# Staging four pairs of attention heads in the room of a later weight matrix: the third and fourth pair brought forward in a fused attention and two-layer expert kernel

## The chip, the cores and the metric

The kernel runs on one core of one Trainium2 chip. The metric is the device time of one execution in microseconds (us), smaller being better; a comparison takes the median of several executions.

## The reference, cut to what matters

```python
def _attn_ref(q, k, v):                      # q, k, v: 4 x 8 x 576 x 64
    scores = scale * np.matmul(q, k.transpose(0, 1, 3, 2))
    kth = np.partition(scores, -top_k, axis=-1)[..., -top_k:-top_k + 1]   # top_k = 32
    scores = np.where(scores >= kth, scores, -1000000000.0)
    attn = softmax(scores)
    return np.matmul(attn, v)
def _moe_ref(x, w_in, w_out):                # x: 2304 x 512, w_in 512 x 2048
    return softplus(x @ w_in) @ w_out
def _moe2_ref(x, w_gate, w1, w2):            # 8 experts, the best one for each token
    return gate * (np.maximum(x @ w1[e], 0) @ w2[e])
```

## The kernel before

The program has three parts that follow and overlap one another: attention with the 32 largest scores of each row kept, a dense layer pair (softplus between the two products), and a layer pair per expert with the tokens sorted by their expert.

**Attention** works on pairs of heads. A pair's q, k and v (each 128 x 576 in float32, 288 KB) are loaded by `load`, called from `prep_load` (L328). `prep_split` (from L375) makes of each a half-precision value and its remainder: ScalarE copies (L386, L406), VectorE or GpSimd subtracts (L387, L407). k and q are then turned by DMA transposes (L389, L392), q is swapped into a second tile by two DMAs (L394, L395), and v is spread over its tile by six DMAs (L411 to L413, twice). ScalarE also sums the magnitudes of each (L343). Pairs 0 to 3 are the four pairs of the first batch and go through `prep_split`; later pairs go through `prep_step` (L440 to L457), a third of a pair at a time. "Pair 2" and "pair 3" below are the third and fourth.

The first four pairs need room that the kernel does not have for long. The weight matrix `w_out_s` (16 blocks of 512 columns in float32) is filled only later, so `load` puts the raw inputs of pair 1 from its block 12 and of pair 2 from its block 8 (`ROOM`), and `staging` puts the halves of pair 1 from its block 4 (`STROOM`). Pairs 0 and 3 use the raw tiles of the pool `raw` (one set, so pair 3's loads wait for pair 0's split, and pair 4's for pair 3's); pairs 0, 2 and 3 use the staging tiles of the pool `stg` (one set, so each waits for the transposes and copies of the one before).

A **group** is two tiles of 128 query rows. PE computes its scores in two pieces (L479, tiles sa and sb), ScalarE copies them out (L489, L525), VectorE folds them and finds the 32nd largest by rounds of MAX8 and MATCH_REPLACE8 (L519 to L545), ScalarE and GpSimd make the exponentials (L552 to L565: Relu with the threshold L553, subtraction L554, Exp L555, half-precision copy L563, remainders L564 and L565), a DMA transpose turns the result (L567, tile pT), and three groups later PE multiplies it with v (L582, L584) and VectorE divides (L606 to L609). There are 72 groups; groups 0 and 1 belong to pair 0, groups 2 and 3 to pair 1, groups 4 and 5 to pair 2, groups 6 and 7 to pair 3.

**The dense layers' weights** arrive as 64-bit numbers and are decoded in 32 blocks (`decode`): a load by SP (L234, two buffers), ScalarE L243 and L247, VectorE L245 and L248, GpSimd L249, and for w_in also L254 to L256. A list `dec_q` holds the blocks in order; `decode_some(n)` takes the next n at a chosen priority. The dense layers run in units of two tiles (L669 first product, L706 and L709 second); a unit starts when the rows of x it needs are done, turned by a DMA transpose (L631, tile xT).

**The order of the work** is not written out. The program text gives each piece a priority (`tc.high_priority(offset=...)`, and `tc.issue_after(x)` holds a piece back until x has been issued), and a scheduler with a timeline of its own lays out one fixed sequence for each engine and for the queue of SP, which issues nearly all DMAs. Each engine then runs its sequence strictly in that order, waiting at an instruction until what it needs is there.

The main loop takes i from -1. At i = -1 it loads pairs 0 and 1, splits those whose time has come, and decodes two blocks; at each later i it emits group i's selection and decodes four blocks (`DECR`). After pair 0's split the loads of pairs 2 and 3 are emitted behind pair 0's last q transpose; after pair 3's split those of pair 4.

Of the kernel before, what the change touches and what calls it, by code (L numbers as in the profile page):

```python
# [19 lines left out]
B, H, S, D = 4, 8, 576, 64  # L20
NT, DM, DFF = 2304, 512, 2048
E, F2 = 8, 1024
R = 9
# [25 lines left out]
SWEEPS = [((0, 1), (8, 2, 3))] * 3 + [((0, 1), (8, 2), (3,))]  # L49
UNITS = [[(b,2*i),(b,2*i+1)] for b in range(3) for i in range(2)]+[[(0,'tail0')],[(3,0),(3,1)],[(3,2),(1,'tail1')],[(3,3)]]  # L50
ROOM = {1: 12, 2: 8}
STROOM = 4
V_NOW = 1
XB = 1
FLB = 4
# [20 lines left out]
DECR = 4  # L76
# [9 lines left out]
A_PREP = 150  # L86
# [110 lines left out]
def part_one(tc, ctx, q, k, v, w_in, w_out, const, ident, before, ones, iota_e, reg_e, wg, ids,  # L197
# [80 lines left out]
    def clear_table():  # L278
        fill = w_out_s[:, KF - 1, DM - (E * NT + SLOT) // 128:].bitcast(I32)
        nc.gpsimd.iota(fill, pattern=[[0, (E * NT + SLOT) // 128]], base=TRASH, channel_multiplier=0)  # L280
        nc.sync.dma_start(table.rearrange("(p a) o -> p (a o)", p=128), fill)
# [28 lines left out]
    def decode_some(n):  # L310
        for _ in range(n):
            if dec_q:
                f, *a = dec_q.pop(0)
                f(*a)


    pair, raws, last_t, last_l = {}, {}, {}, [None]
# [3 lines left out]
    def load(m, i):  # L321
        b, hp = pairs[m]
        if flags is not None and m in ROOM:
            a = ROOM[m] * DM + i * R * D
            t = w_out_s.rearrange("p k c -> p (k c)")[:, a:a + R * D]
        else:
            t = raw.tile([128, R * D], F32, name="qkv"[i] + "n")
        last_l[0] = nc.sync.dma_start(t, (q, k, v)[i][b, 2 * hp:2 * hp + 2].rearrange("h (p r) d -> (h p) (r d)", r=R))  # L328
        pair[m][0][i] = t

    def prep_load(m):
        src = [None] * 3
        bd = sm.tile([128, 3], F32, name="bd") if flags is None else sums[:, m]
        pair[m] = raws[m] = (src, bd)
        for i in range(3):
            load(m, i)
        if flags is None:
            magnitudes(m, stg.tile([128, R * D], F16, name="st"))

    def magnitudes(m, junk):  # L340
        src, bd = raws[m]
        for i, t in enumerate(src):
            nc.scalar.activation(junk, t, AF.Abs, accum_out=bd[:, i:i + 1])  # L343

    def prep_scale(m):
        b = pairs[m][0]
        src, bd = pair[m]
        if flags is not None:
            return
        up, iv = pow2(all_sum(bd, ps_m, "m"), "m")  # L350
        sc = sm.tile([128, 8], F32, name="sc", bufs=KVB + 2)
        nc.vector.tensor_copy(sc[:, 0:3], up)
        nc.vector.tensor_tensor(out=v_up[:, b:b + 1], in0=v_up[:, b:b + 1], in1=up[:, 2:3], op=ALU.min)
        nc.vector.scalar_tensor_tensor(sc[:, 3:4], iv[:, 0:1], 1.0 / D ** 0.5, iv[:, 1:2],
                                       op0=ALU.mult, op1=ALU.mult)
        nc.vector.tensor_scalar(sc[:, 4:5], sc[:, 3:4], -1.0, None, op0=ALU.mult)
        for i in (1, 0, 2):
            nc.scalar.activation(src[i], src[i], AF.Copy, scale=sc[:, i:i + 1])
        pair[m] = (*src, sc)

    def staging(m, i):
        cols = 2 * D + 2 if i == 2 else 2 * D
        if flags is not None and m == 1:
            a = STROOM * DM * 2 + i * R * 2 * D
            st = w_out_s.rearrange("p k c -> p (k c)").bitcast(F16)[:, a:a + R * cols]
            st = st.rearrange("p (r c) -> p r c", c=cols)
        elif i == 2:
            st = stg.tile([128, R, cols], F16, name="vs")
        elif i and m < ST0:
            st = row.tile([128, R, 2, D], F16, name="p16", bufs=PB if flags is not None else 2)  # L370
        else:
            st = stg.tile([128, R, 2, D], F16, name="st")
        return st if i == 2 or len(st.shape) == 4 else st.rearrange("p r (s d) -> p r s d", d=D)

    def prep_split(m):  # L375
        qn, kn, vn, sc = pair[m] if flags is None else (*pair[m][0], None)
        sub = nc.vector if m < DVS else nc.gpsimd
        q1 = kv.tile([128, 2, R, D], F16, name="q1")
        q2 = kv.tile([128, 2, R, D], F16, name="q2")
        kt = kv.tile([128, R, 128], F16, name="kt")  # L380
        if flags is not None and m >= LATEJ:
            magnitudes(m, q2[:, 0].rearrange("p r d -> p (r d)"))
        for i, xs in enumerate((kn, qn)):
            xv = xs.rearrange("p (r d) -> p r d", d=D)
            st = staging(m, i)
            nc.scalar.activation(st[:, :, 0, :], xv, AF.Copy)  # L386
            sub.tensor_tensor(out=st[:, :, 1, :], in0=xv, in1=st[:, :, 0, :], op=ALU.subtract)  # L387
            if i == 0:
                nc.sync.dma_start_transpose(out=kt, in_=st.rearrange("p r s d -> p (r s d)"))  # L389
            else:  # L390
                for h in range(2):
                    last_t[m] = nc.sync.dma_start_transpose(  # L392
                        out=q1[:, h], in_=st[64 * h:64 * h + 64].rearrange("p r s d -> p (r s d)"))
        nc.sync.dma_start(q2[0:64], q1[64:128])  # L394
        nc.sync.dma_start(q2[64:128], q1[0:64])  # L395
        pair[m] = q1, q2, kt, vn, sc
        if V_NOW:
            prep_v(m)
# [321 lines left out]
    def some_work(k):  # L720
        for _ in range(k):
            moe_step()
            if side:
                next(side[0], None)
                if side[0].gi_frame is None:
                    side.pop(0)
# [115 lines left out]
    for b, hp, ts in visits:  # L842
# [3 lines left out]
        m = len(pairs) - 1 - pairs[::-1].index((b, hp))  # L846
# [22 lines left out]
    done_prep, to_scale = 0, []  # L869
    credit, started = 0, 0  # L870
    for i in range(-1, n + LAG):
        if i == -1:
            with tc.high_priority(offset=2 * A_PREP):
                for m in range(RB if flags is None else 2):
                    with ExitStack() as loads_in_order:
                        if m:
                            loads_in_order.enter_context(tc.issue_after(last_l[0].ins))
                        prep_load(m)
                prep_scale(0)
        for m, step in steps.get(i, []):  # L880
            with tc.high_priority(offset=A_PREP):
                prep_step(m, step)
        while done_prep < whole and when[done_prep] <= i:
            with tc.high_priority(offset=A_PREP):
                if to_scale:
                    prep_scale(to_scale.pop()[0])
                prep_split(done_prep)
                if flags is None:
                    if done_prep + RB < len(pairs):
                        prep_load(done_prep + RB)  # L890
                elif done_prep in (0, 3):
                    if done_prep:
                        prep_load(4)
                    else:
                        with tc.issue_after(last_t[0].ins):
                            prep_load(2)
                            prep_load(3)
                if done_prep + 1 < len(pairs):
                    to_scale.append((done_prep + 1, i + SCALE))
            done_prep += 1  # L900
        if to_scale and to_scale[0][1] <= i:
            with tc.high_priority(offset=AHEAD):
                prep_scale(to_scale.pop()[0])
        if i == -1:
            with tc.high_priority(offset=A_PREP), ExitStack() as behind_q:
                behind_q.enter_context(tc.issue_after(last_t[0].ins))
                decode_some(2)
            clear_table()
        if i + 1 < n:
            with tc.high_priority(offset=A_SC):  # L910
                emit_scores(i + 1)
        if 0 <= i < n:
            with tc.high_priority(offset=AHEAD):
                emit_softmax(i)
            with tc.high_priority(offset=0):
                decode_some(DECR)
        j = i - LAG
        if j >= 0:
            with tc.high_priority(offset=A_AV), ExitStack() as behind_scores:
                if i + 1 < n:  # L920

                    behind_scores.enter_context(tc.issue_after(last_qk[0].ins))
                for x in groups[j]:
                    emit_av(*x)
            for u in units.get(j, []):
                started += 1
                ready.append((u, started))
        if ready or cur or behind or side:
            credit += MOER
            some_work(int(credit))  # L930
            credit -= int(credit)
# [270 lines left out]
```

## Time and profile before

| | us |
|---|---|
| median of 3 runs | 1059.6 (1058.11 to 1059.95) |
| the profiled execution | 1056.08 |
| its span, first to last instruction | 1054.1 |
| PE busy in the span | 886.1 (84%) |
| VectorE (DVE) busy | 851.3 (81%) |
| ScalarE (ACT) busy | 802.2 (76%) |
| GpSimd (POOL) busy | 602.0 (57%) |
| first selection (L519) starts | 19.36 |
| a group's first MAX8 (L529) starts, first and last | 21.8 and 688.7 |
| dense layers' first product (L669) starts, first and last | 147.8 and 809.5 |

The shares are means over parts with different limits. In the first 250 us VectorE, ScalarE and GpSimd are nearly always busy and PE mostly waits; from 300 us PE is busy nine tenths of the time and more, to the end. The profiled execution was 3.5 us under the median; the parts of a sum are taken from it and compared with its own time.

### The profile page before, as it was taken

What the parts mean: (1) busy time and instruction counts of PE and PEld (TensorE: products, weight loads), DVE (VectorE), ACT (ScalarE), POOL (GpSimd) and SP (SyncE); (2) the same over time, 40 slices, a digit from 0 to 9 for tenths busy, and PEclk for the clock granted to TensorE, in tenths of its full rate; (3) what the DMA queues carried; (4) which work ended last, traced back from release to release, by engine and by line L of the source; (5) the groups of instructions that cost most, each with busy time, mean ns of one, the idle gap of its engine ahead of it and who ended that gap; (6) DMA issues with size and microseconds to landing.
All of it is one profiled execution on the core that took longest, in us unless ns stands there. A gap on an engine that the chain in (4) does not pass through costs nothing.

```text
span 1054.1 us, 22206 instructions
## 1 busy us (share of the span) xinstructions
PE 886.1 (84%) x7146; PEld 657.8 (62%) x7146; DVE 851.3 (81%) x3021; ACT 802.2 (76%) x1866; POOL 602.0 (57%) x631
## 2 busy tenths in 40 slices
PE   2124359775999998998999899999999999999995
PEld 1013246444766666665667566676787899999993
DVE  4879999898989798996998999955457887777774
ACT  5879889989879898997997898863678455555553
POOL 3789989898768787876787677661001022111111
PEclk9965569886999998998999999999999999999998
DMA  8897889977698996769879456465101667766760
GB/s 198 204 219 167 179 183 213 197 168 148 98 142 160 156 161 117 125 91 152 149 125 118 80 90 99 69 102 180 37 16 26 170 218 241 244 218 220 235 216 23
DMA packets 295859, 156.97 MB, mean 149 GB/s; under 512 B 257524, under 2 KB 257652, under 8 KB 295732
## 3 DMA queue, kind: packets, MB, share of 16 engines
q1 hardware_dynamic: 292116, 145.73, 66.4%
q0 software_dynamic: 3616, 9.72, 2.6%
q8 instruction: 58, 0.95, 0.4%
q14 instruction: 69, 0.57, 0.2%
HBM read 77.89 MB, written 11.11 MB: 84 GB/s over the span
## 4 chain that ended last, share of the span: by engine, by line
PE 50%; DVE 18%; DMA 8%; ACT 8%; POOL 7%; issue 5%; SPq 3%; POOLq 0%; ACTq 0%; DVEq 0%
PE h L1033 10%; PE y L1046 10%; PE h L669 10%; PE y L709 9%; DVE mx L545 5%; DVE wk L541 4%; PE y L706 3%; POOL e L554 2%; PE m L582 2%; DMA xT<-xh 2%; PE sb L479 2%; POOL p L565 2%; DMA kt<-st 1%; DVE wk L524 1%; DMA w<-in_moe_w_out_dram 1%
## 5 line engine op out<-in xcount | busy, mean ns | idle before, releaser
L709 PE MATMUL y<-w_out_s,g 128*128 128x512 f32 x480 | 233.7, 610 | 1.8 <-ACT g L684 1.5
L669 PE MATMUL h<-xT,w_in_s 128*128 128x256 f16 (+1 forms) x1920 | 219.7, 264 | 14.5 <-ACT sa L683 7.1
L669 PEld LDWEIGHTS <-w_in_s 128*128 128x128 f16 x1920 | 172.8, 100 | 70.9 <-issue 49.1
L554 POOL TENSOR_TENSOR e<-s,e 128x576 f32<-128x576 f32 x144 | 202.9, 1428 | 19.8 <-ACT e L553 12.7
L545 DVE MAX8 mx<-wk 128x8 f32<-128x128 f32 (+2 forms) x432 | 200.3, 500 | 0.1
L565 POOL TENSOR_TENSOR p<-e,p 128x512 f16<-128x512 f32 x144 | 167.2, 1161 | 0.0
L479 PEld LDWEIGHTS <-q 128*128 128x128 f16 (+1 forms) x640 | 55.6, 108 | 178.5 <-issue 139.1
L541 DVE MATCH_REPLACE8 wk<-mx,wk 128x128 f32<-128x128 f32 (+1 forms) x432 | 144.4, 340 | 0.1
L709 PEld LDWEIGHTS y<-w_out_s,g 128*128 128x128 f32 x480 | 83.8, 195 | 65.4 <-issue 57.7
L1013 POOL DMA_INDIRECT out_dram<-ot,idx x19 | 19.6, 1029 | 178.9 <-DVE ot L1012 176.1
L479 PE MATMUL sb<-kt,q 128*128 128x320 f16 (+1 forms) x320 | 62.2, 337 | 66.4 <-ACT s L525 66.2
L555 ACT ACTIVATE e<-e,bias 128x576 f32<-128x576 f32 x144 | 110.5, 769 | 9.5 <-POOL e L554 9.0
L1046 PE MATMUL y<-wf,hT 128*128 128x512 f32 x432 | 114.5, 403 | 1.4 <-DVE ohcum L770 1.4
L1033 PEld LDWEIGHTS h<-xT,wf 128*128 128x128 f32 x864 | 111.8, 191 | 5.4 <-ACT wf L994 0.2
L1033 PE MATMUL h<-xT,wf 128*128 128x256 f32 x864 | 113.9, 283 | 0.0
L553 ACT ACTIVATE e<-s,kths 128x576 f32<-128x576 f32 x144 | 105.6, 769 | 1.9 <-POOL p L565 0.7
L479 PE MATMUL sa<-kt,q 128*128 128x256 f16 (+1 forms) x320 | 53.1, 306 | 61.3 <-ACT s L489 36.6
L582 PEld LDWEIGHTS <-pT 128*128 128x128 f16 (+1 forms) x1440 | 88.5, 107 | 20.8 <-issue 17.2
L582 PE MATMUL m<-v,pT 128*128 128x65 f16 (+1 forms) x1440 | 95.4, 203 | 7.0 <-DVE xtail L609 3.6
L563 ACT ACTIVATE p<-e 128x576 f16<-128x576 f32 x144 | 97.5, 679 | 0.8
L1046 PEld LDWEIGHTS y<-wf,hT 128*128 128x128 f32 x432 | 77.8, 191 | 15.0 <-DVE ohcum L770 1.5
L564 POOL TENSOR_TENSOR p<-e,p 128x64 f16<-128x64 f32 x144 | 45.3, 315 | 69.9 <-ACT p L563 61.3
(245 smaller groups left out, 1794.8 us busy)
## 6 DMA issues: line engine op xcount, KB each, us to landing
w1r<-in_moe_w_dram SPq DMA_DIRECT2D x20, 1024.0 KB
w2r<-in_moe_w_dram SPq DMA_DIRECT2D x20, 1024.0 KB
w<-in_moe_w_in_dram SPq DMA_DIRECT2D x16, 512.0 KB
w<-in_moe_w_out_dram SPq DMA_DIRECT2D x16, 512.0 KB
rows<-xr SPq DMA_DIRECT2D x37, 128.2 KB
q<-q SPq DMA_DIRECT2D x32, 144.0 KB
qn<-in_q_dram SPq DMA_DIRECT2D x14, 288.0 KB
kn<-in_k_dram SPq DMA_DIRECT2D x14, 288.0 KB
```

Source lines behind the costliest of these rows:

```text
L479: last_qk[0] = nc.tensor.matmul(ps[p0:p1], lhsT=qs[:, h, r0:r1, :].rearrange("p r d -> p (r d)"), rhs=kt[:, k0:k1, cs], start=first, stop= ...
L541: nc.vector.match_replace(out=to, in_to_replace=mx[:, i, 8 * j:8 * j + 8], in_values=src[i], imm_value=NEG)
L545: nc.vector.max(out=mx[:, i, 8 * j + 8:8 * j + 16], in_=src[i])
L553: nc.scalar.activation(e[i], s[i], AF.Relu, bias=kths[:, 2 * gi + i], scale=-K_UP)
L554: nc.gpsimd.tensor_tensor(out=e[i], in0=s[i], in1=e[i], op=ALU.subtract)
L555: nc.scalar.activation(e[i], e[i], AF.Exp, bias=bt[:, i], scale=SCORE)
L565: nc.gpsimd.tensor_tensor(out=p16[:, S + D:], in0=e[i][:, 0:S - D], in1=p16[:, 0:S - D], op=ALU.subtract)
L582: nc.tensor.matmul(o[:, h, 0:D + 1], lhsT=pT(r), rhs=v16[:, h, c, 0:D + 1], start=r == 0, stop=r == R - 1)
L669: nc.tensor.matmul(hps[:, :n], lhsT=w_in_s[:, c, j, p, o:o + 128], rhs=xT[:, 0:len(u.tiles), r, c, :], start=m == 0, stop=m == 3 * KD - 1)
L709: nc.tensor.matmul(u.y[i], lhsT=g[:, cs], rhs=w_out_s[:, f, :], start=f == 0, stop=f == KF - 1)
L1033: nc.tensor.matmul(h, lhsT=w1f[:, a, c, :], rhs=xT[:, b, c, :], start=n == 0, stop=n == 3 * KD - 1)
L1046: nc.tensor.matmul(y[i], lhsT=hT[g][:, a, i * 128:i * 128 + 128], rhs=w2f[:, b, :], start=g == 0 and n == 0, stop=g == KF2 - 1 and n == 2)
```

## The change

`STROOM` becomes a table: the halves of pair 2 are staged from block 12 of `w_out_s`, where the raw inputs of pair 1 lay, and those of pair 3 from block 8, where those of pair 2 lay. The pool `stg` then serves pair 0 and the later pairs alone. The loads of pairs 2 and 3 are no longer emitted after pair 0's split but after pair 1's, behind its last q transpose and at twice the priority offset. At i = -1 four blocks of weights are decoded at preparation priority instead of two, and at i = 0 two instead of four.

```diff
-STROOM = 4
+STROOM = {1: 4, 2: 12, 3: 8}
...
-        if flags is not None and m == 1:
-            a = STROOM * DM * 2 + i * R * 2 * D
+        if flags is not None and m in STROOM:
+            a = STROOM[m] * DM * 2 + i * R * 2 * D
...
-                elif done_prep in (0, 3):
-                    if done_prep:
-                        prep_load(4)
-                    else:
-                        with tc.issue_after(last_t[0].ins):
-                            prep_load(2)
-                            prep_load(3)
+                elif done_prep == 3:
+                    prep_load(4)
+                elif done_prep == 1:
+                    with tc.high_priority(offset=2 * A_PREP), tc.issue_after(last_t[1].ins):
+                        prep_load(2)
+                        prep_load(3)
...
-                decode_some(2)
+                decode_some(4)
...
-                decode_some(DECR)
+                decode_some(DECR if i else 2)
```

The scheduler lays out all sequences anew. Three places are shown; numbers behind names tell tiles of one kind apart.

On the queue of SP, around the first transposes of the exponentials (pT). Before, the six v copies of pair 2 end here (v_388), the two pT of group 0 follow, then the fifth block of weights and pair 2's q transposes:

```order
L412 DMA v_388<-vs 64x4x130
L413 DMA v_388<-vs 64x130
L567 DMA_TRANSPOSE pT<-p_315 128x9x128
L567 DMA_TRANSPOSE pT<-p_321 128x9x128
L234 DMA w<-in_moe_w_out_dram 128x1024
L392 DMA_TRANSPOSE q_371<-st 128x9x64 x2
L394 DMA q_372<-q_371 64x1152
L395 DMA q_372<-q_371 64x1152
```

Now, with all transposes and v copies of the four pairs issued above this place (p_341 and p_347 are group 0's, p_441 and p_447 group 1's, p_542 the first of group 2; the upper block of weights is the fourth, the lower one the fifth; the loads of kn and vn below the four transposes are those of pair 5):

```order
L328 DMA kn<-in_k_dram 128x576
L328 DMA vn<-in_v_dram 128x576
L234 DMA w<-in_moe_w_in_dram 128x1024
L567 DMA_TRANSPOSE pT<-p_341 128x9x128
L567 DMA_TRANSPOSE pT<-p_347 128x9x128
L567 DMA_TRANSPOSE pT<-p_441 128x9x128
L567 DMA_TRANSPOSE pT<-p_447 128x9x128
L328 DMA kn<-in_k_dram 128x576
L328 DMA vn<-in_v_dram 128x576
L567 DMA_TRANSPOSE pT<-p_542 128x9x128
L281 DMA table<-w_out_s 128x146
L234 DMA w<-in_moe_w_out_dram 128x1024
```

All preparation of pairs 2 and 3 has moved ahead of the first pT, and the fifth block of weights from behind group 0's second pT to behind group 2's first.

On VectorE, from the end of the fifth group (group 4) to the start of the sixth (L519). Before, seven blocks are decoded ahead of group 4 and the eighth here:

```order
L541 MATCH_REPLACE wk<-mx,wk 128x320 x2
L245 TENSOR_SCALAR y<-y 128x512
L545 MAX mx<-wk 128x8 x2
L606 TENSOR_SCALAR rc<-m 128x2
L519 TENSOR_TENSOR sb<-sb,s 128x2x128
L248 SCALAR_TENSOR_TENSOR xr<-w,y 128x512
```

Now three are decoded ahead of the end of group 4, and the fourth and fifth stand between it and group 5:

```order
L545 MAX mx<-wk 128x8 x2
L245 TENSOR_SCALAR y<-y 128x512
L248 SCALAR_TENSOR_TENSOR xr<-w,y 128x512
L606 TENSOR_SCALAR rc<-m 128x2
L608 RECIPROCAL rc<-rc 128x2
L609 TENSOR_TENSOR x_758<-m,rc 128x128
L606 TENSOR_SCALAR rc<-m 128x2
L608 RECIPROCAL rc<-rc 128x2
L609 TENSOR_TENSOR x_890<-m,rc 128x128
L245 TENSOR_SCALAR y<-y 128x512
L248 SCALAR_TENSOR_TENSOR xr<-w,y 128x512
L519 TENSOR_TENSOR sb<-sb,s 128x2x128
```

At the start of group 5 eight blocks stood decoded (the eighth by half) and now five.

On the queue of SP again, at the second xT of the second dense unit. Before:

```order
L457 DMA v_3025<-vs 64x130
L567 DMA_TRANSPOSE pT<-p_2798 128x9x128
L631 DMA_TRANSPOSE xT<-xh 128x8x128
L567 DMA_TRANSPOSE pT<-p_2804 128x9x128
L567 DMA_TRANSPOSE pT<-p_2918 128x9x128
```

Now:

```order
L457 DMA v_3019<-vs 64x130
L567 DMA_TRANSPOSE pT<-p_2792 128x9x128
L567 DMA_TRANSPOSE pT<-p_2798 128x9x128
L631 DMA_TRANSPOSE xT<-xh 128x8x128
L328 DMA qn<-in_q_dram 128x576
```

The xT has moved behind the second pT of that group.

## Rows read from the trace of the kernel before

**Rows 1.** By stretch: busy PE, PEld, DVE, ACT, POOL, granted clock, DMA share, GB/s.

```profile
25.00:50.00 25.00, 3.60 (x14) 1.61 (x12) 21.45 (x70) 21.51 (x48) 17.73 (x19) 1.00 0.83 205
50.00:75.00 25.00, 7.54 (x73) 5.13 (x73) 19.40 (x66) 18.93 (x36) 21.76 (x23) 0.70 0.95 209
75.00:100.00 25.00, 10.86 (x109) 7.54 (x108) 24.69 (x90) 23.76 (x47) 23.92 (x24) 0.57 0.86 191
...
200.00:250.00 50.00, 32.76 (x260) 20.61 (x260) 42.58 (x135) 44.19 (x97) 44.65 (x45) 0.74 0.82 176
250.00:300.00 50.00, 45.95 (x420) 33.01 (x420) 48.61 (x205) 45.17 (x105) 41.09 (x45) 0.92 0.82 136
300.00:400.00 100.00, 94.08 (x808) 62.14 (x807) 86.46 (x356) 87.48 (x215) 76.59 (x84) 1.00 0.93 149
```

**Rows 2.** Timeline of VectorE, 19 to 67 us: start, us, ..., [idle before <-releaser].

```profile
19.36 0.43 DVE L519 TENSOR_TENSOR sb<-sb,s 128x256 f32<-128x256 f32 x1 [3.21 <-ACT s L489]
...
25.15 0.43 DVE L519 TENSOR_TENSOR sb<-sb,s 128x256 f32<-128x256 f32 x1 [0.82 <-PE sb L479]
...
48.82 0.70 DVE L245 TENSOR_SCALAR y<-y 128x512 uint32<-128x512 uint32 x1 [2.85 <-ACT y L243]
...
50.21 0.42 DVE L519 TENSOR_TENSOR sb<-sb,s 128x256 f32<-128x256 f32 x1
...
52.07 0.68 DVE L524 TENSOR_TENSOR wk<-sb,s 128x512 f32<-128x512 f32 x1
...
56.19 1.41 DVE L545 MAX8 mx<-wk 128x8 f32<-128x576 f32 x2
...
60.74 0.70 DVE L245 TENSOR_SCALAR y<-y 128x512 uint32<-128x512 uint32 x1 [2.84 <-ACT y L243]
61.34 0.28 DVE L609 TENSOR_TENSOR x<-m,rc 128x128 f32<-128x128 f32 x1
...
63.13 0.70 DVE L245 TENSOR_SCALAR y<-y 128x512 uint32<-128x512 uint32 x1 [0.91 <-ACT y L243]
...
66.10 0.43 DVE L519 TENSOR_TENSOR sb<-sb,s 128x256 f32<-128x256 f32 x1 [1.48 <-ACT s L489]
```

**Rows 3.** Timeline of ScalarE, 48 to 63 us.

```profile
48.16 0.62 ACT L243 ACTIVATE y<-w 128x512 f32<-128x512 f32 x1 [0.20 <-DMA w<-in_moe_w_out_dram]
...
58.66 0.68 ACT L440 ACTIVATE vs<-vn 128x576 f16<-128x576 f32 x1 [2.71 <-DMA vn<-in_v_dram]
...
60.08 0.63 ACT L243 ACTIVATE y<-w 128x512 f32<-128x512 f32 x1
...
62.47 0.63 ACT L243 ACTIVATE y<-w 128x512 f32<-128x512 f32 x1 [1.08 <-DMA w<-in_moe_w_out_dram]
```

**Rows 4.** Timeline of SP's queue, 20 to 44 us; the duration is the issue's.

```profile
20.88 0.62 SPq L411 DMA_DIRECT2D v<-w_out_s  x1
...
40.55 2.73 SPq L567 DMA_TRANSPOSE pT<-p  x2
43.37 0.64 SPq L234 DMA_DIRECT2D w<-in_moe_w_out_dram  x1
```

**Rows 5.** Timeline of GpSimd, 61 to 70 us.

```profile
61.24 1.26 POOL L442 TENSOR_TENSOR vs<-vn,vs 128x576 f16<-128x576 f32 x1
...
69.64 0.30 POOL L564 TENSOR_TENSOR p<-e,p 128x64 f16<-128x64 f32 x1
69.90 1.16 POOL L565 TENSOR_TENSOR p<-e,p 128x512 f16<-128x512 f32 x1
```

**Rows 6.** Timeline of SP's queue, 254 to 257 us.

```profile
254.31 1.28 SPq L631 DMA_TRANSPOSE xT<-xh  x1
256.21 2.71 SPq L567 DMA_TRANSPOSE pT<-p  x2
```

**Rows 7.** Timeline of PE at the start of the second dense unit.

```profile
257.49 2.73 PE L669 MATMUL h<-xT,w_in_s 128*128 128x256 f16 x21 [0.38 <-DMA xT<-xh]
```

**Rows 8.** Chain of waits, the longest stretch of plain issue after 300 us.

```profile
575.05 5.35 issue
```

## The prediction

> **What bounds the kernel now.** I read the busy time by stretch first, then each engine's timeline where VectorE stands idle, then the chain of waits. By stretches VectorE is the busiest engine of the first 250 us: 24.69 of 25 us from 75 to 100, but only 21.45 and 19.40 in the two stretches before, and 42.58 of 50 from 200 to 250 [rows 1]. From 300 us PE carries the load, 94.08 of 100. The change touches the two stretches in which VectorE has holes. The reader should see there that an engine which has the most work is still made to wait, since its sequence is fixed.
>
> VectorE's timeline names the holes [rows 2]: 0.82 before group 1, 2.85 before the fifth weight block, 2.84 and 0.91 before the sixth and seventh, 1.48 before group 4, together 8.9 us. The first three of the later ones end at ScalarE's L243, and ScalarE itself was waiting for a DMA: for a block of weights, for pair 4's v (2.71 us), for a block again (1.08) [rows 3]. So what ends last is a transfer that SP issued late. SP spends 0.62 us on a v copy and 1.37 on a pT (2.73 for two), and these stand before the weights [rows 4].
>
> **The change, part by part.** The same instructions run on every engine, so only their places count. One group costs VectorE 7.4 us without a block (L519 at 50.21 to the last MAX8's end at 57.60) and one block 1.39 (48.82 to 50.21) [rows 2].
>
> *Removed.* The five holes go, since pairs 2 and 3 are prepared by about 32 us and nothing of the first four groups waits for a block that is late: 8.9 us. This is the most that can be won here.
>
> *Six loads moved on SP ahead of the second block of weights and of pair 1's swaps.* They push both back by under 3 us. VectorE needs the second block only inside group 1 and pair 1 only in group 2, at 36 us; I cost this at nothing. Without that cover group 1 would pay up to 3 us.
>
> *Preparation of two pairs on GpSimd ahead of group 0's exponentials.* Six subtractions of 1.26 us, as L442's [rows 5], and the second block's addition now stand before group 0's L554; group 2's copy of scores reuses the buffer that L554 reads. VectorE ends group 1 at 19.4 + 2 x 7.4 + 1.4 = 35.6. GpSimd gets the second block at about 31.7 (group 1's start at 26.8, 2.5 of folding, 0.9 of maxima, 1.4 of the block), needs 3 x 1.26 more, ScalarE 0.6 for the copy: 36.1. A new wait of 0.6 us; bounds 0 and 1.7.
>
> *The third block's load* stands behind all transposes and some twenty v copies. GpSimd ends pair 3's q at about 28.7; then three transposes of 1.37, 1.5 us until the last has landed, one swap and thirteen v copies at 0.66 bring the issue to 43.5, its data to 48.3 (43.37 to 48.16 in [rows 3, 4], 4.8 us) and VectorE's part to 49.0. VectorE reaches it in group 3, 4.5 us after 43.6, at 48.1. I charge 0.9; bounds 0 and 2.
>
> *The fifth block's load*, now behind group 2's first pT, is the large term. VectorE can't start group 5 before it, and the way to it starts in group 4. From group 4's L519: folding 2.5 us (50.21 to the end of L524 at 52.75); ScalarE's L525, L531 and then pair 4's third of a preparation, nine instructions of 0.6 to 0.8, 5.3 (L440 and L441 take 1.42, 58.66 to 60.08 [rows 3]); GpSimd's second L442 and group 2's L564 and L565, 2.6 [rows 5]; SP's pT and the table's fill, 2.0 [rows 4]; the transfer 4.8; L243 0.66 and the block itself 1.39 [rows 2, 3]. Sum 19.2. VectorE has work for 7.4 + 1.4 + 1.4 of it, and two divisions of three short instructions, none over L609's 0.28 [rows 2]: I take 0.9 of at most 1.7. So it stands idle 8.1 us. Lower bound 6.1, if SP's 2.0 vanish; upper 10.8, if pair 4's load is late again by the 2.71 of [rows 3].
>
> *Debt.* At group 5 five blocks are decoded where eight were: 3 x 1.39 = 4.2 us that VectorE still owes. It is counted as work that must be done, not as gain, since the stretch after it is full (24.69 of 25).
>
> *The xT of the second dense unit* leaves SP behind one more pT: at 257.56 (256.21 + 1.35) in place of 254.31 [rows 6], 3.3 us. PE starts that unit when it lands [rows 7]. I take none of it in the forecast: from 250 to 300 VectorE is busy 48.61 of 50 and paces the groups while PE has 4 us to spare [rows 1], so a later start can be caught up. Bounds 0 and 3.3.
>
> Sum: -8.9 + 0.6 + 0.9 + 8.1 = +0.7 us. The profiled execution gives 1056.1 + 0.7 = 1056.8; it was 3.5 us under the median, so the median comes to **1060.3**, no change.
>
> *A rule against a row.* SP's rows show 0.62 us for a copy and 1.37 for a transpose, one after the other, with nothing between [rows 4]; that is how a load came late. The Trainium skill, "DMA: Bandwidth & Descriptors", section "Issuing engines are not separate DMA queues", holds instead that the time a sequencer takes to initiate a DMA "is usually small relative to the DMA itself". By it the sum would lose SP's terms and read -2.2 in place of +0.7; the rows here disagree.
>
> **The rivals.**
>
> *The debt costs nothing (faster).* VectorE is idle 7.4 us from 200 to 250 [rows 1]. If the three blocks fall into such holes, group 5 and all after it run 4.2 - 0.7 = 3.5 us earlier, PE's full stretch starts as much earlier, and the median is 1056.1. For it: the holes are there, and ScalarE and GpSimd are no fuller than VectorE. Against it: from 75 to 100 all three are near full, and the holes at 200 come when the last blocks are read.
>
> *The xT decides (slower).* PE has next to no dense work between the first and the second unit, and from 300 us it is the bound. If the second unit starts 3.3 us late and PE then has no slack, the end moves by it: 1063.6. It decides as soon as the first product of that unit starts later than about 261 us (257.5 + 3.3) in a run whose groups are on time. For it: the chain of waits goes through this very transfer [rows 7]. Against it: the slack of 4 us up to 300.
>
> *SP's issue is not what delays.* If, for whatever reason, the DMAs behind one another cost no time on SP, the chain to the fifth block loses 2.0 us and the third block's 0.9 goes: -2.2, 1057.4. It is what the Trainium skill's sentence above amounts to. For it: pT's 2.73 include some waiting perhaps. Against it: v copies follow at even distances in the same timeline.
>
> That the change does not do what it says can be left out: in the new sequences the six loads and all transposes of pairs 2 and 3 stand ahead of the first pT.
>
> **How the numbers follow.** A measurement of this kernel tells 0.2%, 2.1 us, from no change. After 250 us the whole order is laid out anew, for which I allow one stall like the longest one, 5.35 us [rows 8], either way. Chances: forecast 0.32 (of it faster 0.08, same 0.15, slower 0.09); debt free 0.29 (0.23, 0.05, 0.01); xT 0.27 (0, 0.05, 0.22); SP free 0.12 (0.05, 0.05, 0.02). Together faster 0.36, same 0.30, slower 0.34. The range goes from the debt-free case less 5.3, 1051, to the xT case plus 5.3, 1069. The forecast's own range, by the bounds of its terms (0 to 1.7, 0 to 2, 6.1 to 10.8, 0 to 3.3), is 1056 to 1069 less what can't come together, some 1057 to 1065.
>
> **What would show it.** Right: VectorE without a hole over 2 us from 26 to 60 us; group 4 started by about 53 us and not 66; a hole of 6 to 11 us on VectorE before group 5, ended by ScalarE's L243 and behind it a load of w_out; group 5 started near 72 us, five blocks done. Wrong: no such hole, or group 5 before 68 us; a hole in group 1 (then the moved loads cost what I set at nothing); the second dense unit's first product over 4 us from 257.5 [rows 7] with the early part as I say (then the debt, or the xT, is the step that failed).

## The result, and the profile after

The changed kernel took 1070.06 us (median of 4 runs, 1068.56 to 1074.76) where the kernel before took 1059.08 on the same chip (4 runs): ratio 1.0105, 95% interval 1.0078 to 1.0132. It is slower by 11 us; the forecast was no change at 1060.3, with a range up to 1069. The profiled execution of the change took 1070.82 us, its span 1068.8.

Busy time of the change in three of the stretches of [rows 1], same columns:

```profile
50.00:75.00 25.00, 6.43 (x67) 4.47 (x67) 15.36 (x48) 17.69 (x35) 16.89 (x16) 1.00 0.97 204
...
250.00:300.00 50.00, 39.05 (x365) 27.88 (x364) 49.18 (x197) 42.94 (x97) 41.28 (x46) 0.90 0.68 133
300.00:400.00 100.00, 86.34 (x738) 57.62 (x737) 79.87 (x335) 78.56 (x193) 68.28 (x73) 0.97 0.75 129
```

The third number is PE: from 250 to 400 us it did 125.4 us of work where it did 140.0 before. The fifth is VectorE: 15.36 of 25 us from 50 to 75, where it was 19.40.

VectorE's timeline, to set beside [rows 2]:

```profile
50.37 0.70 DVE L245 TENSOR_SCALAR y<-y 128x512 uint32<-128x512 uint32 x1 [3.57 <-ACT y L243]
53.28 0.42 DVE L519 TENSOR_TENSOR sb<-sb,s 128x256 f32<-128x256 f32 x1
...
66.60 0.16 DVE L606 TENSOR_SCALAR rc<-m 128x2 f32<-128x2 f32 x1 [2.06 <-PE m L582]
73.47 0.70 DVE L245 TENSOR_SCALAR y<-y 128x512 uint32<-128x512 uint32 x1 [6.18 <-ACT y L243]
74.87 0.42 DVE L519 TENSOR_TENSOR sb<-sb,s 128x256 f32<-128x256 f32 x1
```

Group 4 starts at 53.28 and group 5 at 74.87, with a hole of 6.18 us between them that ends at the fifth block of weights. ScalarE and SP behind those holes, to set beside [rows 3, 4]:

```profile
49.72 0.62 ACT L243 ACTIVATE y<-w 128x512 f32<-128x512 f32 x1 [3.84 <-DMA w<-in_moe_w_in_dram]
72.81 0.63 ACT L243 ACTIVATE y<-w 128x512 f32<-128x512 f32 x1 [2.83 <-DMA w<-in_moe_w_out_dram]
```

```profile
44.77 0.56 SPq L234 DMA_DIRECT2D w<-in_moe_w_in_dram  x1
55.02 8.60 SPq L567 DMA_TRANSPOSE pT<-p  x4
67.81 1.35 SPq L234 DMA_DIRECT2D w<-in_moe_w_out_dram  x1
```

So far the change does nearly what was foretold: the hole of 3.57 us stands where none over 2 us was expected, and group 5 starts 2.9 us later than the 72 us forecast. The second dense unit, to set beside [rows 6, 7]:

```profile
266.47 4.33 PE L669 MATMUL h<-xT,w_in_s 128*128 128x256 f16 x24 [1.11 <-DMA xT<-xh]
```

It starts 9.0 us later than before.

**Where the time went.** I cut VectorE's timeline at the starts of groups 0, 6 and 20 (L519) and summed its gaps. Up to group 20 both kernels run the same 644 VectorE instructions, 31 blocks of weights among them; the change takes 231.7 us and the kernel before 222.3. All of it is idle time: 29.5 us against 20.2. Of the 9.3 more, 4.5 lie ahead of group 6 and 4.8 behind it, most of these in groups 10 to 14:

```profile
135.65 0.43 DVE L519 TENSOR_TENSOR sb<-sb,s 128x256 f32<-128x256 f32 x1 [0.72 <-ACT s L489]
...
140.75 1.65 DVE L245 TENSOR_SCALAR xr<-xr 128x512 uint32<-128x512 uint32 x1 [1.26 <-POOL xh L630]
...
160.45 0.91 DVE L245 TENSOR_SCALAR xr<-xr 128x512 uint32<-128x512 uint32 x1 [1.36 <-ACT xr L243]
...
175.85 0.43 DVE L519 TENSOR_TENSOR sb<-sb,s 128x256 f32<-128x256 f32 x1 [2.07 <-ACT s L489]
```

Behind group 20 the distance still grows. The change starts that group 8.4 us later than the kernel before and the last group 16.1 us later; the two profiled executions lie 14.7 us apart in their spans, where the medians lie 11.0 apart.

### The profile page after: what moved, and what is told of

It reads as the page before. It is cut to its first block, busy times and chain, and to the rows that moved or that the text cites. A ratio compares the mean times of both kernels' runs of the same rounds, so it can differ in the third digit from the quotient of the medians.

```text
span 1068.8 us, 22203 instructions
## 1 busy us (share of the span) xinstructions
PE 888.8 (83%) x7146; PEld 656.8 (61%) x7146; DVE 853.3 (80%) x3021; ACT 801.8 (75%) x1866; POOL 604.6 (57%) x631
## 4 chain that ended last, share of the span: by engine, by line
PE 44%; DVE 15%; ACT 13%; DMA 10%; POOL 8%; issue 5%; SPq 4%; POOLq 0%; ACTq 0%; DVEq 0%
PE y L1045 9%; PE h L1032 9%; PE h L669 8%; PE y L709 7%; DVE mx L545 3%; PE y L706 3%; DVE wk L541 3%; POOL e L554 3%; DMA q<-w 2%; POOL p L565 2%; DMA w<-in_moe_w_in_dram 2%; DMA pT<-p 2%; ACT e L553 2%; ACT e L555 2%; ACT p L563 1%
## 5 line engine op out<-in xcount | busy, mean ns | idle before, releaser
L669 PE MATMUL h<-xT,w_in_s 128*128 128x256 f16 (+1 forms) x1920 | 227.6, 269 | 22.9 <-ACT sa L683 7.6
L709 PE MATMUL y<-w_out_s,g 128*128 128x512 f32 x480 | 231.6, 605 | 12.9 <-ACT g L684 11.9
L669 PEld LDWEIGHTS <-w_in_s 128*128 128x128 f16 x1920 | 174.9, 101 | 86.0 <-issue 49.7
L479 PEld LDWEIGHTS <-q 128*128 128x128 f16 (+1 forms) x640 | 55.8, 108 | 167.9 <-issue 132.1
L582 PE MATMUL m<-v,pT 128*128 128x65 f16 (+1 forms) x1440 | 94.6, 201 | 10.4 <-DMA pT<-p 5.8
L582 PEld LDWEIGHTS <-pT 128*128 128x128 f16 (+1 forms) x1440 | 87.1, 106 | 26.0 <-issue 15.2
L1045 PEld LDWEIGHTS y<-wf,hT 128*128 128x128 f32 x432 | 76.7, 189 | 13.3 <-DVE ohcum L770 0.3
```

Of the source, the lines that this page charges most:

```text
L479: last_qk[0] = nc.tensor.matmul(ps[p0:p1], lhsT=qs[:, h, r0:r1, :].rearrange("p r d -> p (r d)"), rhs=kt[:, k0:k1, cs], start=first, stop= ...
L582: nc.tensor.matmul(o[:, h, 0:D + 1], lhsT=pT(r), rhs=v16[:, h, c, 0:D + 1], start=r == 0, stop=r == R - 1)
L669: nc.tensor.matmul(hps[:, :n], lhsT=w_in_s[:, c, j, p, o:o + 128], rhs=xT[:, 0:len(u.tiles), r, c, :], start=m == 0, stop=m == 3 * KD - 1)
L709: nc.tensor.matmul(u.y[i], lhsT=g[:, cs], rhs=w_out_s[:, f, :], start=f == 0, stop=f == KF - 1)
L1045: nc.tensor.matmul(y[i], lhsT=hT[g][:, a, i * 128:i * 128 + 128], rhs=w2f[:, b, :], start=g == 0 and n == 0, stop=g == KF2 - 1 and n == 2)
```

## The experiments

The first theories were three. *Queue theory*: transposes and v copies of pairs 2 and 3 crowd SP ahead of the first pT and the weights. *Blocks theory*: the blocks' new priority does it. *Order theory*: any edit has the scheduler lay the sequences anew, and that alone moves the time. "Measured" gives the time as a ratio to the kernel before, which ran on the same chip, with its 95% interval in brackets; 0.001 is about 1.1 us. It rests on 4 to 12 executions of each kernel, against 17 to 23 of the kernel before. A profile shows one execution.

### Parts of the change

The two parts alone, the change without the blocks' edit, and the change with the v copies of pairs 2 and 3 held behind the first pT:

```diff
 # blocks alone: the kernel before, with
-                decode_some(2)
+                decode_some(4)
...
-                decode_some(DECR)
+                decode_some(DECR if i else 2)
 # staging alone: the kernel before, with
-STROOM = 4
+STROOM = {1: 4, 2: 12, 3: 8}
...
 # v behind pT: the change, with (last_pt[i] is group i's pT)
...
-        if V_NOW:
+        if V_NOW and flags is not None and m in (2, 3):
+            with tc.issue_after(last_pt[m - 2].ins):
+                prep_v(m)
+        elif V_NOW:
```

Blocks alone. 

> Before, with only the change of the weights' blocks (four at the first step, two at the next). Queue theory (the transposes and v copies of pairs 2 and 3 crowd SP's queue ahead of the first pT and the weights): nothing is crowded here, so VectorE's holes up to 75 us stay near 9 us, the second dense unit starts at 257 +-5 and the time is 1056 to 1063. Blocks theory (the loss comes from the blocks' new priority): second unit 5 us late or more, 1066 or more. Order theory (any edit lays the order after 250 us out anew and that alone moves the time): early part as before, the end anywhere within 10 us.

Measured: 1.0052 (1.0031 to 1.0073), 5.5 us; by the ratio that is between the first two theories' ranges.

Staging alone. 

> Before, with only the new places of staging (pairs 2 and 3 in the old raw inputs' room); loads and blocks as before. In its order all kt transposes stand ahead of the first pT, as in the change. Queue theory: holes of 12 us or more up to 75 us, second unit at 262 or later, 1065 to 1073. Blocks theory: as before, 1056 to 1062. Order theory: early part not decisive, the end anywhere within 10 us of 1059.

Measured: 1.0019 (0.9997 to 1.0041).

Without the blocks' edit. 

> The change with the blocks as before (two at the first step, four at the next); staging and loads changed. The third block now stands behind group 3's first pT on SP. Queue theory: as slow as the change or slower, second unit at 264 or later, 1067 to 1076. Blocks theory: 1056 to 1062. Order theory: anywhere within 10 us of 1065.

Measured: 1.0090 (1.0056 to 1.0123). The loss is there without the blocks' edit, so the blocks theory fails. Staging alone, with all transposes ahead of the first pT, loses about 2 us, and the queue theory asked for 6 or more.

v behind pT. 

> The change with the halving and copies of v of pair 2 held behind group 0's pT and of pair 3 behind group 1's: 12 DMAs leave the place ahead of the first pT on SP. Queue theory: first pT at about 47 us and not 55, the hole before group 5 down to 4 us or less, second unit at 261 or earlier, 1056 to 1065. Blocks theory: no better than the change, 1067 to 1073. Order theory: the early part better, the end anywhere within 10 us.

Measured: 1.0077 (1.0044 to 1.0111). VectorE's idle time ahead of group 6 was 8.5 us, less than the 10.0 of before, and still the kernel was slow. In this kernel the first holes are not the loss.

### Halves of the order

The kernel before ran beside each of these kernels; its median went from 1052.9 to 1059.1 us by chip, so ratios are compared and not times. From here on some kernels have their sequences set by a table:

```diff
+        if halves:
+            pin_late(tc)
```

`pin_late` lays an "issue after" edge from each instruction of the table to the one ahead of it on its engine; nothing else is touched. Lines of such a kernel's profile are two higher.

New front, old rest. 

> The change's order up to the start of group 6 (its sixth selection is the last free one), and from there on, on every engine and on SP, exactly the sequence of the kernel before; same instructions, only places. Front theory (what the change does in the first 75 us, its later holes and the three blocks of weights it still owes, is the loss): ratio to before 1.007 to 1.012, second dense unit's first product at 263 us or later. Order theory (the sequence that the scheduler lays out anew behind group 6 is the loss, whatever stood in front): ratio 0.997 to 1.003, second unit at 257 to 260.

Measured: 1.0089 (1.0069 to 1.0110).

Old front, new rest. 

> The counterpart: the order of the kernel before up to the start of group 6, and from there on the sequence of the changed kernel. Front theory: ratio 0.997 to 1.003, second unit's first product by 259 us. Order theory: ratio 1.006 to 1.012, second unit at 262 us or later, although nothing of the change itself is in it.

Measured: 1.0084 (1.0062 to 1.0106).

New order up to group 20. 

> The change's order up to the start of group 20 (about 250 us), the sequence of before from there on. If the loss lies before group 20, in front or in the order between 75 and 250 us: ratio 1.005 to 1.012, second unit at 262 or later, and the distance to before no longer grows behind it. If it lies in the order after 250 us (the second xT, the zero fill, the third and fourth unit): ratio 0.998 to 1.004.

Measured: 1.0116 (1.0093 to 1.0138). With the old order from group 20 on, the old place of the second xT with it, the whole loss is there, so what causes it stands ahead of group 20. Not all of it shows there, though: the distance to the kernel before, which was expected to grow no longer, is 7.8 us at the start of group 20 and 16.3 us at that of the last group.

Each half alone loses nearly all, so neither theory holds as it stood. What the two halves share is six blocks of weights decoded at group 6 where before there were nine. In the first of them the debt can be watched. The three blocks that it owes are done in groups 6 and 7, and VectorE idles 5.6 us more there than before. All of it stands before L245, here L247, and the longest piece is this:

```profile
94.75 0.70 DVE L247 TENSOR_SCALAR y<-y 128x512 uint32<-128x512 uint32 x1 [3.22 <-ACT y L245]
```

From group 8 on it owes nothing and follows the order of before, and it stays 7 to 9 us behind up to group 30.

Two orders laid anew by a priority offset alone (`A_SC` 97, then 110, in place of 100):

Null, late. 

> The kernel before with one priority offset set from 100 to 97: no part of the change, the same sequences up to about the 27th group, others behind it. Order theory: the time moves by 2 us or more either way (ratio outside 0.998 to 1.002). Front theory: ratio 0.998 to 1.002.

Measured: 0.9976 (0.9959 to 0.9994).

Null, early. 

> The kernel before with one priority offset set from 100 to 110: no part of the change, same order up to group 11 or 12, another behind it. Order theory (what the scheduler lays out between groups 10 and 20 by chance decides): idle time of VectorE from group 10 to 14 rises from 1.3 to 4 us or more, ratio 1.003 or more. Front or debt theory: ratio 0.997 to 1.002.

Measured: 1.0010 (0.9993 to 1.0028); idle time in groups 10 to 14 was 1.4 us. In these two, laying the order anew is worth 1 to 3 us, not 11; the 5.5 us of blocks alone say that it can be more.

### Weights placed by hand, and loads moved on SP

Debt by hand. 

> The kernel before in its own order on every engine, but the sixth to eighth block of weights are taken out of the first 75 us and three places for blocks are added between the 13th and 25th, so that VectorE owes three blocks at group 5 as in the change; nothing else moves. Debt theory (a block done later, where VectorE, ScalarE and GpSimd are all full, costs more than the 1.39 us it saves in front): ratio 1.004 to 1.008. If the debt is paid in holes or costs what it saves: 0.997 to 1.002.

Measured: 1.0297 (1.0277 to 1.0317), far more than any theory said: my places were poor ones, and VectorE idles 22.9 us in groups 10 to 14 alone.

New front, debt spread by hand. 

> The change's order up to group 6, the order of before behind it, and the three owed blocks at places spread between the 14th and 26th block instead of all at once behind group 6. Front theory (only the holes of the first 75 us remain, idle time of VectorE up to group 6 13 to 14.5 us and to group 20 23 to 25): ratio 1.003 to 1.006. Debt theory: 1.007 to 1.011, as much as the change. If the loss is the newly laid order between groups 6 and 20 alone: 0.998 to 1.003.

Measured: 1.0342 (1.0320 to 1.0365). The two show one thing well: 33.7 and 41.5 us more idle time up to group 20 than before, and medians that are 32.3 and 38.3 us longer. In these two kernels idle time of VectorE there is not caught up.

Four loads of weights earlier, in the change. 

> The changed kernel in exactly its own order on all engines; on SP alone four loads of weights are issued earlier: the third block's ahead of all but one of the v copies, the fourth's ahead of the last eight, the fifth's behind the first pT instead of the fifth, the sixth's ahead of the sixth pT. Front theory (SP's queue ahead of those loads is what the two large holes wait for): the hole of 3.6 us at 47 us goes, the 9.1 us before group 5 fall to 4 to 6.5, group 6 starts 4 to 7 us earlier than in the change, and the whole is 1.004 to 1.007 of before instead of 1.0105. If the holes of the front do not reach the end: 1.009 to 1.012.

Measured: 1.0100 (1.0070 to 1.0131). The 3.57 us hole went and idle time ahead of group 6 fell from 14.5 to 10.4, but the time is that of the change as far as the interval tells. One of the six executions, 1076.29 us, lies 8.6 us above the next and lifts the ratio; the medians alone give 1.0084.

The same with pair 4's inputs. 

> The changed kernel in its own order on all engines; on SP the four loads of weights are earlier as in the run before, and the three inputs of pair 4 are issued ahead of the last 15 v copies instead of behind all. If idle time in front goes to the end one for one: VectorE's idle time up to group 6 falls from 14.5 us to 6 to 9, group 6 starts at 73 to 77 us, and the ratio to before is 1.003 to 1.006. If the loss sits behind group 6 alone: ratio still 1.008 to 1.012.

Measured: 1.0115 (1.0073 to 1.0156), idle time ahead of group 6 11.4.

Loads earlier in the kernel before. 

> The kernel before in its own order on all engines; on SP alone pair 4's v and the sixth and seventh block's load are issued ahead of pair 3's v copies (the seventh behind four of them). One for one: the holes of 2.84, 0.91 and 1.48 us at 58 to 66 us shrink by 3 to 4 us and the ratio is 0.995 to 0.998. If idle time in front is caught up later: 0.999 to 1.002.

Measured: 1.0038 (1.0022 to 1.0055), a miss: idle time ahead of group 6 was 10.6 us, not 6 to 7. ScalarE at the place of [rows 3] where it had waited 2.71 us for pair 4's v (L442 here is L440):

```profile
60.12 0.68 ACT L442 ACTIVATE vs<-vn 128x576 f16<-128x576 f32 x1 [4.77 <-DMA v<-vs]
```

The loads came in time, and the v copies behind them came late: SP issued the last of them at 56.38 us where it had been at 54.70. The hole changed its name and stayed. Why this kernel loses 4 us stays open, since from group 6 to group 20 VectorE idles no more than before.

Both together. 

> The order re-laid behind the 27th group (ratio 0.9976) with the same three loads earlier on SP. If the two add: 0.992 to 0.997. If the re-laid order's gain was scatter: 0.996 to 1.000.

Measured: 1.0013 (0.9993 to 1.0033). The gain of the late null is not kept here, so no kernel of this study is surely faster than the one before.

### The debt, laid out by the scheduler

```diff
 # the kernel before (last_pt[0] is the last pT emitted); larger debt: (3, 0, 0)[i], held at i == 3
...
-                decode_some(DECR)
+                n_dec = (4, 0, 4)[i] if i < 3 else DECR
+                if n_dec:
+                    with ExitStack() as behind_p:
+                        if i == 2:
+                            behind_p.enter_context(tc.issue_after(last_pt[0].ins))
+                        decode_some(n_dec)
 # less debt: the change, with
-                decode_some(4)
+                decode_some(8)
...
-                decode_some(DECR if i else 2)
+                decode_some(DECR if i > 1 else 1)
```

Debt. 

> The kernel before, nothing of the change in it, with the decoding of the seventh block and all later ones held back behind group 2's last pT, so that six blocks stand decoded at group 6 instead of nine and two are still owed at groups 9 to 16, about as in the change (six; one to two owed). Debt theory: ratio 1.006 to 1.011. If the debt is paid in holes: 0.998 to 1.003.

Measured: 1.0036 (1.0014 to 1.0059): a loss, but under the range.

Larger debt. 

> The same, held back more: five blocks decoded at group 6 instead of nine and two to three owed up to group 18. Debt theory: more than the run before it, ratio 1.009 to 1.016. If the debt is paid in holes: 0.998 to 1.003.

Measured: 1.0128 (1.0098 to 1.0159). Nothing of the change is in this kernel, and it loses as much as the change or more.

The change with less debt. 

> The change with eight blocks of weights instead of four at preparation priority: eight blocks decoded at group 6 instead of six (before: nine), one owed after that. Debt theory: ratio 1.002 to 1.006. If the loss is the front's holes or the newly laid order: 1.008 to 1.012.

Measured: 1.0004 (0.9982 to 1.0026). At the start of group 6 seven blocks are done and the eighth is half done, the rest of the change's program text is kept, and the 11 us are gone, more than the debt theory's range allowed. The order is laid anew here too. Its holes ahead of group 6 are still there (12.8 us). PE's rows for 250 to 300 and 300 to 400 us in this kernel:

```profile
250.00:300.00 50.00, 39.91 (x370) 28.26 (x369) 48.51 (x195) 44.97 (x100) 41.55 (x48) 0.90 0.77 129
300.00:400.00 100.00, 91.95 (x770) 61.95 (x770) 82.69 (x343) 83.31 (x203) 73.81 (x78) 0.95 0.93 150
```

From 250 to 400 us PE does 131.9 us of work, between the change's 125.4 and the 140.0 of before. The second dense unit starts as late as the change's, and that does not hurt:

```profile
266.59 3.31 PE L669 MATMUL h<-xT,w_in_s 128*128 128x256 f16 x23
```

All profiled runs together, by idle time of VectorE from group 6 to group 20 (gaps summed between the L519 of both):

| kernel | blocks begun by group 6 | idle to group 6 | idle 6 to 20 | ratio |
|---|---|---|---|---|
| null, early | 9 | 8.6 | 8.2 | 1.0010 |
| change, less debt | 8 | 12.8 | 8.4 | 1.0004 |
| null, late | 9 | 9.5 | 8.7 | 0.9976 |
| before, loads earlier | 9 | 10.6 | 9.7 | 1.0038 |
| null and loads | 9 | 11.2 | 9.7 | 1.0013 |
| before | 9 | 10.0 | 10.2 | 1 |
| staging alone | 7 | 12.2 | 11.9 | 1.0019 |
| blocks alone | 11 | 12.6 | 12.1 | 1.0052 |
| new front, old rest | 6 | 13.3 | 13.4 | 1.0089 |
| change, loads earlier | 6 | 10.4 | 14.6 | 1.0100 |
| the change | 6 | 14.5 | 15.0 | 1.0105 |
| new to group 20 | 6 | 13.2 | 15.2 | 1.0116 |
| v behind pT | 5 | 8.5 | 16.0 | 1.0077 |
| old front, new rest | 6 | 11.9 | 16.1 | 1.0084 |
| debt | 6 | 9.5 | 16.2 | 1.0036 |
| change, loads earlier, pair 4 too | 6 | 11.4 | 17.5 | 1.0115 |
| without the blocks' edit | 4 | 10.8 | 20.1 | 1.0090 |
| larger debt | 5 | 9.8 | 20.6 | 1.0128 |
| debt by hand | 6 | 10.9 | 43.0 | 1.0297 |
| new front, debt by hand | 6 | 13.4 | 48.3 | 1.0342 |

The fourth column sorts the ratios roughly, to within some 5 us; the third does not sort them at all. Every kernel with six blocks or fewer begun by group 6 idles 13 us or more behind it, every one with seven or more 12.1 or less.

That makes late blocks a sign of the loss, but the column is not its price. Each idle time is that of one execution, which lay up to 6.4 us from the median of its kernel (null, early). Blocks alone owes nothing and idles 12.1 us. Without the blocks' edit, with four blocks, loses no more than the change with six. And larger debt, v behind pT and the kernel without the blocks' edit start group 20 ahead of the kernel before, by 0.8 to 1.8 us with none to three blocks still owed, and fall behind only then, by 9 to 17 us at group 40.

In the change the late blocks show on PE too. The waits of the first product (L669) from 140 to 250 us for the two halves of a decoded block, in the change (engine, line waited for: us in total, times, longest):

```profile
PE h L669 <- ACT w_in_s L255: 7.4, 3, 3.9
...
PE h L669 <- POOL w_in_s L256: 4.7, 4, 1.7
```

In the kernel before, and then in the change with less debt:

```profile
PE h L669 <- POOL w_in_s L256: 2.4, 1, 2.4
...
PE h L669 <- ACT w_in_s L255: 2.3, 1, 2.3
```

```profile
PE h L669 <- ACT w_in_s L255: 4.2, 3, 3.3
```

12.1 us, 4.7 and 4.2. The first dense unit stands in PE's sequence among the scores and reads each block of w_in soon after it is made. When the blocks are late, PE stands still there, and what is behind it in the sequence waits with it.

This is not the path in general. Larger debt, which loses no less, has these lines, one higher in its numbering:

```profile
PE h L670 <- ACT w_in_s L256: 5.2, 3, 2.4
...
PE h L670 <- POOL w_in_s L257: 1.5, 1, 1.5
```

That is 6.7 us. New front, old rest has 5.7, and v behind pT has 3.4, which is less than the 4.7 of before. PE's waits on all lines in this stretch sum to 30.7 us in the change and 31.6 before. By which path late blocks cost the time at the end is not shown.

## Why the prediction was wrong

**The step that failed is the debt.** "Debt: ... 3 x 1.39 = 4.2 us that VectorE still owes. It is counted as work that must be done, not as gain" took it that three blocks done later cost what they had cost in front. From group 6 to group 20 the kernel before takes 158.4 us with 23 blocks, the change 167.9 with 26: 9.5 us for three blocks, 3.2 each, 1.39 of them work and the rest waits that were not there before. New front, old rest shows the same in two groups: 5.6 us of idle time on top of the work of the three. Larger debt shows the loss without the change, less debt shows the change without the loss; both are also orders laid anew, and the runs that moved blocks alone, by hand, had poor places for them. So that the late blocks and nothing else make the 11 us is argued and not shown.

Of the 9.3 us more that VectorE idles up to group 20 the forecast had 0.7, in front. The waits of the debt are 4.8, and the holes in front are 3.8 larger than forecast, most of it the third block's.

No fixed price per block comes out of this. In the same groups the kernel under "Debt" does 25 blocks in 158.9 us, two more than before in 0.6 us more, and larger debt does 25 in 162.7. Why "Debt", with the same six blocks at group 6, lost only 4 us, and why the change falls from 8.4 to 16.1 us behind after group 20, stays open.

**Removed holes, 8.9 us: right, and not what decides.** Group 4 started at 53.28 (about 53 was forecast). But v behind pT had less idle time in front than the kernel before and lost 8 us, and less debt has 12.8 us of it and loses nothing.

**Six loads moved, 0: right**; no hole above 1 us stands in group 1. **Group 2's wait, 0.6:** 0.97, within its bounds. **Third block, 0.9 (0 to 2): mis-sized**, 3.57. The load was issued at 44.77 for the forecast 43.5, ScalarE's L243 followed 4.95 us later, and VectorE was ready at 46.8 rather than 48.1. **Fifth block, 8.1 (6.1 to 10.8): right**, 0.77 + 2.06 + 6.18 = 9.0 before group 5, with five blocks done; SP's four pT took 8.60 us, where [rows 4] have 2.73 for two, and the way from group 4's start to group 5's took 21.6 us for the 19.2 of the sum. Together these make the 4.5 us of idle time ahead of group 6 where I had 0.7. How much of those reaches the end stays open: taking 4.1 away left the ratio where it was within its interval, while the medians fell by about 2 us.

**The xT, 0 in the forecast: right, and the rival wrong.** The unit did start past its 261 us, so by the text either the debt or the xT had failed. With xT's old place the loss stayed (new to group 20), and with the unit at 266.59 the change with less debt is level with the kernel before. The slack of which I wrote is real for that unit.

**The debt-free rival** is wrong for the same reason as the forecast. It also misread [rows 1]: from 200 to 250 us ScalarE and GpSimd, with 44.19 and 44.65 of 50, are fuller than VectorE with 42.58. In three of the four stretches that those rows show of the first 250 us another engine is busier than VectorE. **SP's issue is not what delays** is not borne out. With four loads earlier in the change, the third block's ahead of nearly all v copies, the hole of 3.57 us went. In the kernel before, two loads issued 4 to 5 us earlier and a third issued one earlier shortened nothing in sum, but there the v copies behind them were issued later and came late. The Trainium skill, "DMA: Bandwidth & Descriptors", section "Issuing engines are not separate DMA queues", says that all transfers run on the same 16 DMA engines and interleave; the 0.95 busy share of these from 50 to 75 us [rows 1] and the hole that moved from vn to the v copies agree with the sharing. These are transfers of SP alone, so no run here shows it for DMAs that different engines issue.

**The 5.35 us allowed for a re-laid order** was fair: by their ratios the two nulls gave -2.5 and +1.1 us, and blocks alone 5.5.

## What to carry to other kernels

When work of low priority is pushed out of a stretch with holes, ask who reads its result and stands in a fixed sequence with other work; do not price it by its own instructions alone: here three blocks of 1.39 us cost 9.5 us in one order, and two cost 0.6 and 4.4 us in others. Before judging an edit of a scheduled kernel, measure one or two edits that only lay the order anew, since they show how much of a difference is scatter. A hole's releaser names the transfer that came last, which need not be the one to move: moving loads forward took 4.1 us of holes away in the change, and in the kernel before it only moved the hole to the next transfer.

## What the runs showed of the hardware

I had not expected how little an earlier issue brought in the kernel before. With the DMA engines busy 0.87 of 30 to 75 us in that run (0.95 of 50 to 75 us before), three loads issued one to five us earlier turned a wait of 2.71 us for one transfer into 4.77 us for another. The semaphore events in the trace of the change show what a small copy pays behind a load on the same queue: the v copies issued from 45.37 to 47.99 us, right behind the third block's load of 512 KB, land 4.5 to 2.6 us after their issue, one after the other from 49.9 us, and ScalarE starts on that block at 49.72; the copies issued ahead of the load land after 1.9 to 2.4 us. Nor had I expected that idle time of one engine in the first quarter is passed on nearly whole (33.7 us became 32.3, 41.5 became 38.3, in the two kernels by hand) in a kernel that PE bounds from 300 us on.
